# Attention with a sliding window: V held in small array tiles, its product turned on VectorE, and corner masks as products

## The chip, the cores and the metric

One core of one Trainium2 chip runs the whole kernel. The metric is device time in microseconds, the median of several executions; lower is better. The kernel before took 478.73 us (median of three, 477.96 to 478.87).

## What is computed

Two layers over 2048 rows of 512 features. Each layer is an attention block and a dense block, both with a residual and a layer norm ahead of them:

```python
def _A_ref(x, wqkv, wo):                 # H = 32 heads of Dh = 16, window W = 256
    qkv = (x @ wqkv).reshape(B, S, 3, H, Dh)   # then q, k, v as (B, H, S, Dh)
    scores = einsum("bhqd,bhkd->bhqk", q, k) * Dh ** -0.5
    mask = (q_index - k_index >= 0) & (q_index - k_index < W)
    p = softmax(where(mask, scores, -1e9))
    return einsum("bhqk,bhkd->bhqd", p, v)  # heads joined again, then @ wo

def _B_ref(x, w1, w2):                   # Dff = 1792
    return maximum(x @ w1, 0) @ w2

x = x + _A_ref(layernorm(x), wqkv, wo)
x = x + _B_ref(layernorm(x), w1, w2)     # and both once more
```

Inputs and result are bf16; sums are kept in fp32.

## The kernel before, in words

The work goes in eight steps `k`, four chunks of 512 rows for each of the two layers. A step has a norm and q, k, v (`plan_qkv`), attention (`plan_attention`), the projection with `wo`, a second norm and the dense block (`plan_rest`).

**Attention.** The 32 heads are taken in four sets `t` of eight; the eight are four pairs `p` (or `r`) of two heads `e`. A `Unit` is one set over the 512 queries of a step, 28 of them in all; step 0 has eight half units of 256 queries instead. Keys and queries are cut into blocks of 64. A query block sees five key blocks (fewer at the start of the sequence), so a full unit away from the start has 40 pairs of a key block and a query block; all units together have 1200. The tables `FULL`, `HALF` and `BARE` pack these pairs into groups: an entry `(kb, lo, n, at)` is key block `kb` with the `n` query blocks from `lo` on, laid at column `64 * at`. All units together have 372 such entries.

A group is one step of a pipeline. `score_group` makes four matmuls per entry, each on 32 rows of the array (a pair `r`), whose stationary operand `KBD` holds the keys of both heads, so that the result `Sps` has two times 64 keys in its 128 partitions and the queries in its columns. `Sps` fills four PSUM banks and there is one of it, so the scores of the next group wait for the exponential of this one. `exp_group` writes the exponentials to `Pb` (line 418), of which there are two, used by every second unit. Corners, the blocks that the window cuts in a triangle, are set to zero by `mask` (line 422): VectorE takes the minimum with a triangle of 0 and 3e38, a pair of corners in one instruction; GpSimd makes a select for each corner and each head, so four for a pair. All units together have 480 corners.

`pv_group` (line 445) is the attention product. The stationary operand is a 128x128 piece of `Pb` (two heads by 64 keys, 128 queries), the moving one is `V2` with 34 columns: 16 features and a one for each of the two heads, with zeros where the other head's keys lie. The sums build up over up to six key blocks in `acc`, with queries in the partitions; the columns of ones give the softmax sums. A unit is done in pieces of 256 queries, each with one PSUM bank. `divide` (line 453) takes reciprocals of the sums and writes the quotients to `O`. When all four sets of a step are done, four DMA transposes from SP's queue turn `O` into `OT` (in the last step TensorE does it), and `wo` is applied. `accumulate_check` (line 462) keeps whether a reciprocal lay outside fixed bounds; a slow exact path at the end of the program runs if one did.

**The order of the work** is worked out when the program is built. Each piece of work is an `Op` with its engines, a duration for each of them written in the source, what it depends on, and the PSUM bank or buffer it takes (`psum`, four banks, for everything but the scores). A list scheduler walks through time: an idle engine takes the ready piece with the lowest key (for TensorE the key alone; for the others the time since when it is ready, plus a key). Scores come first on TensorE, then the attention product, then the projection, then the dense matmuls by their due times. Where two engines can do a piece (masks: VectorE or GpSimd; evacuations of PSUM: VectorE or ScalarE), the one that is idle first takes it. ScalarE takes other work only if it ends before the next exponential is due (`act_free`). If TensorE has been idle for 0.81 us, a filler matmul (`warm`) is put in. Every engine then runs its instructions in the order so found; the durations in the source only make the order. As every instruction is issued through one helper, nearly all have line 150 in the profile, so they are told apart by tile names.

Of the kernel before, what the change touches and what calls it, by code (L numbers as in the profile page):

```python
# [14 lines left out]
ALU = mybir.AluOpType  # L15
# [24 lines left out]
PW = 576  # L40
# [36 lines left out]
SHOW = None  # L77


class Unit:  # L80


    def __init__(self, k, c, t, q0, nq):
# [4 lines left out]
        self.place = {(kb, q // 2): (g, lo, at) for g, blocks in enumerate(self.groups) for kb, lo, n, at in blocks  # L88
                      for q in range(lo, lo + n)}
# [17 lines left out]
def kernel(  # L107
# [22 lines left out]
    BIG = 3.0e38  # L130
# [75 lines left out]
    Pb = [const.tile([P, PWALL + 64], BF16, name=f"Pb{i}") for i in range(2)]  # L206
    badacc = const.tile([P, 1], FP32, name="badacc")
# [59 lines left out]
    def op(key, opts, deps=(), take=None, uses=(), keep=0):  # L267
        uses = list(uses) + ([take] if take is not None and take not in uses else [])
        return Op(key, opts, deps, take, uses, keep)
# [4 lines left out]
    ots = Pool("OT", 3, work)  # L274

    def landed(t):
        o = Op(0, {}, [], None, [], 0)
        fixed.append((o, t))
        return o
# [116 lines left out]
    def spread_v(e, layer, c, j, src):  # L396
        v4 = src.rearrange("p (a e d) -> p e a d", e=2, d=16)
        for half in range(2):
            sl = slot(layer, 8 * c + 2 * j + half)
            for p in range(2):  # L400
                copy(e, V2[64 * p:64 * p + 64, sl, p, :, 0:16], v4[64 * half:64 * half + 64, p])
# [13 lines left out]
    def places(pb, g):  # L415
        return Pb[pb][:, 0:PWALL].rearrange("p (g r c) -> p g r c", g=5, r=4)[:, g]

    def exp_group(u, g, pb, Sps):
        a, z = bounds(u, g)
        act.activation(places(pb, g)[:, :, 64 + a:64 + z], Sps[:, :, a:z], ACT.Exp, scale=0.25)  # L420

    def mask(e, m, pv4):
        if e == "POOL":
            for at, far in m:
                for h in range(2):
                    v = pv4[64 * h:64 * h + 64, :, 64 + 64 * at:128 + 64 * at]
                    pool.affine_select(out=v, in_=v, pattern=[[0, 4], [-1 if far else 1, 64]],
                                       compare_op=ALU.is_gt if far else ALU.is_ge, fill=0.0, base=0,
                                       channel_multiplier=1 if far else -1)
            return  # L430
        at, k0 = m[0]
        if len(m) == 1:
            v = pv4[:, :, 64 + 64 * at:128 + 64 * at]
            w = tri[:, k0:k0 + 1, :].to_broadcast([P, 4, 64])
        else:
            st, k1 = m[1][0] - at, m[1][1]
            b = pv4[:, :, 64 + 64 * at:128 + 64 * at]
# [4 lines left out]
    def seen(u, jl):  # L442
# [584 lines left out]
```

## Time and profile before

| | |
|---|---|
| median of three runs | 478.73 us (477.96 to 478.87) |
| span of the profiled execution | 474.6 us (its time around the span is not given) |
| busy in the span: TensorE, VectorE, ScalarE, GpSimd | 451.7, 348.1, 345.9, 299.4 us |
| instructions | 14227 |

The span runs from the first to the last instruction of the profiled execution. PE is TensorE's matmuls, PEld its weight loads, DVE VectorE, ACT ScalarE, POOL GpSimd, SP SyncE; a queue of an engine has a q behind it. A row of a group of instructions gives engine, operation, tiles (out<-in), shapes, the count, busy time and the mean duration of one in ns, then the engine's idle time before them and what ended it. Matmuls overlap, so their mean duration holds a latency that a row of them pays once.

### The profile page before, as it was taken

To read this page: it belongs to the slowest core of one execution; us is meant where nothing else is said; L and a number is where in the kernel's file an instruction comes from. 1 tells how busy PE (TensorE), PEld (TensorE's weight loads), DVE (VectorE), ACT (ScalarE), POOL (GpSimd) and SP (SyncE) were. 2 spreads that over 40 slices of the span, in tenths; PEclk is the share of its full clock that TensorE was granted. 3 is DMA by queue.
4 is the path that set the end of the run, shared out by engine and by line. 5 is a ranking of instruction groups with operands and counts; after the bars stand their busy time and mean duration, and the time that the engine had idled before them with its cause. 6 is when DMAs were issued, how large, how long until landed. Compare 5 with 4: busy or idle time off the path is not lost.

```text
span 474.6 us, 14227 instructions
## 1 busy us (share of the span) xinstructions
PE 451.7 (95%) x5890; PEld 242.8 (51%) x5963; DVE 348.1 (73%) x845; ACT 345.9 (73%) x277; POOL 299.4 (63%) x664
## 2 busy tenths in 40 slices
PE   6988999999999999999999999999999999999994
PEld 2654556554555554545454555455555555644443
DVE  6898997887896689767979866898779766461101
ACT  1887987887889778887788787888788788444330
POOL 7587678786797678666887576687767756410000
PEclk9999999999999999999999999999999999999999
DMA  8617122013111112002232022020242002100101
GB/s 267 244 35 192 23 46 48 1 35 47 26 32 36 23 36 46 3 1 47 44 48 35 14 46 46 1 48 3 41 73 46 12 15 35 46 12 11 35 12 39
DMA packets 54807, 21.96 MB, mean 46 GB/s; under 512 B 46160, under 2 KB 54224, under 8 KB 54736
## 3 DMA queue, kind: packets, MB, share of 16 engines
q1 hardware_dynamic: 54736, 20.98, 19.9%
q8 instruction: 48, 0.79, 0.7%
q14 instruction: 23, 0.19, 0.1%
HBM read 7.86 MB, written 2.10 MB: 21 GB/s over the span
## 4 chain that ended last, share of the span: by engine, by line
PE 82%; ACT 5%; DVE 5%; DMA 3%; issue 3%; POOL 2%; SPq 0%; ACTq 0%; DVEq 0%; POOLq 0%
PE ps_d L150 59%; PE acc L150 13%; PE Sps L150 9%; ACT Pb L150 4%; DMA OT<-O 2%; DVE V2f L150 1%; POOL Pb L150 1%; DMA xnT<-xn 1%; DMA x_sb<-in_A_x_dram 1%; PE tp L150 1%; DVE st L150 1%; DVE Pb L150 0%; DVE Vst L150 0%; POOL rstds L150 0%; DVE xn L150 0%
## 5 line engine op out<-in xcount | busy, mean ns | idle before, releaser
L150 ACT ACTIVATE Pb<-Sps 128x2048 bf16<-128x2048 f32 (+2 forms) x156 | 282.6, 1811 | 66.9 <-PE Sps L150 52.2
L150 POOL TENSOR_SCALAR_AFFINE_SELECT Pb<-Pb 64x256 bf16<-64x256 bf16 x504 | 221.8, 440 | 98.5 <-ACT Pb L150 72.2
L150 PE MATMUL ps_d<-xn2T,w 128*128 128x512 bf16 (+1 forms) x485 | 104.7, 355 | 1.6 <-issue 0.8
L150 PE MATMUL ps_d<-w,hT 128*128 128x512 bf16 (+1 forms) x438 | 103.5, 373 | 2.1 <-issue 1.4
L150 PEld LDWEIGHTS <-Pb 128*128 128x128 bf16 x2880 | 82.9, 96 | 21.3 <-issue 9.4
L150 PE MATMUL acc<-V2f,Pb 128*128 128x34 bf16 x2880 | 88.3, 178 | 0.7 <-POOL Pb L150 0.3
L150 DVE TENSOR_TENSOR Pb<-Pb,tri 128x256 bf16<-128x256 bf16 (+1 forms) x143 | 59.9, 429 | 16.9 <-ACT Pb L150 15.6
L150 PEld LDWEIGHTS <-w 128*128 128x128 bf16 x504 | 45.9, 98 | 44.2 <-issue 4.2
L150 PE MATMUL ps_d<-xnT,wqkv 128*128 128x512 bf16 (+1 forms) x275 | 63.3, 355 | 2.3 <-DMA xnT<-xn 1.2
L150 PEld LDWEIGHTS <-hT 128*128 128x128 bf16 x462 | 42.1, 98 | 45.5 <-issue 4.2
L150 PE MATMUL Sps<-Qt,KBD 32*128 32x320 bf16 (+3 forms) x1488 | 60.9, 251 | 3.9 <-ACT Pb L150 3.0
L150 DVE TENSOR_SCALAR hT<-ps_d 128x512 bf16<-128x512 f32 (+1 forms) x66 | 39.6, 607 | 16.4 <-PE ps_d L150 15.7
L150 ACT ACTIVATE hT<-ps_d 128x512 bf16<-128x512 f32 (+1 forms) x60 | 33.9, 568 | 23.5 <-PE ps_d L150 22.2
L150 PEld LDWEIGHTS <-KBD 32*128 32x128 bf16 x1488 | 23.4, 92 | 51.9 <-issue 49.0
L150 DVE TENSOR_SCALAR KBD<-ps_d,par 128x256 bf16<-128x256 f32 (+1 forms) x80 | 44.0, 601 | 1.6 <-PE ps_d L150 1.3
L150 DVE BATCH_NORM_STATS2 st<-x_sb 128x6 f32<-128x512 f32 (+1 forms) x64 | 43.7, 683 | 1.0 <-DMA x_sb<-in_A_x_dram 0.7
L150 DVE TENSOR_TENSOR x_sb<-ps_d,x_sb 128x512 f32<-128x512 f32 x48 | 32.4, 683 | 10.4 <-PE ps_d L150 9.3
L150 PEld LDWEIGHTS <-wqkv 128*128 128x128 bf16 x288 | 25.3, 97 | 25.3 <-issue 4.8
L150 DVE TENSOR_TENSOR ob<-ps_d,x_sb 128x512 bf16<-128x512 f32 (+1 forms) x17 | 11.2, 659 | 32.8 <-PE ps_d L150 32.2
L150 POOL TENSOR_TENSOR rstds<-rstds,mhalf 128x2 f32<-128x2 f32 (+1 forms) x33 | 24.3, 739 | 16.4 <-DVE rstds L150 13.5
L150 DVE TENSOR_SCALAR xn<-x_sb,mvs,rstds 128x512 bf16<-128x512 f32 (+1 forms) x45 | 25.0, 575 | 13.2 <-issue 9.3
L150 PE MATMUL ps_d<-wo,OT 128*128 128x512 bf16 x118 | 31.3, 380 | 1.9 <-DMA OT<-O 1.2
(56 smaller groups left out, 285.1 us busy)
## 6 DMA issues: line engine op xcount, KB each, us to landing
out_dram<-ob SPq DMA_DIRECT2D x15, 128.0 KB, 1.7
w<-in_B_w_dram SPq DMA_DIRECT2D x1, 1792.0 KB, 12.0
w<-in_B_w_dram SPq DMA_DIRECT2D x2, 896.0 KB, 6.4
wqkv<-in_A_wqkv_dram SPq DMA_DIRECT2D x3, 512.0 KB, 7.1
x_sb<-in_A_x_dram SPq DMA_DIRECT2D x3, 512.0 KB, 9.0
x_sb<-in_A_x_dram SPq DMA_DIRECT2D x2, 256.0 KB, 3.0
wo<-in_A_wo_dram SPq DMA_DIRECT2D x1, 512.0 KB, 8.8
xnT<-xn SPq DMA_TRANSPOSE x28, 2.5
```

The source lines that it names most:

```text
L150: inst = fn(*a, **k)
```

## The change

The attention product is turned round: V is the stationary operand, in tiles of 64 rows by 32 columns of the array, one for each of the eight heads of a set, and the exponentials are the moving operand, with up to 320 columns. The result has features in its partitions (for each of four pairs 32, of which 17 are used) and queries in its columns, in two PSUM banks, one for each `e`; a unit takes both at once and is done in one piece. VectorE turns both banks in blocks of 32x32 into fp32 tiles in SBUF, takes reciprocals and the quotients, and turns the quotients back into `OT`, whose layout is that of the transposed `O`; `O`, its DMA transposes and TensorE's transposes in the last step go. GpSimd masks as VectorE does, a pair of corners in one instruction; both multiply by a triangle of 0 and 1. The check now compares each reciprocal with both bounds, so that one that is not a number counts as bad. `V2` needs no zeros and `Pb` no padding any more. The scheduler can take two banks for one piece of work. The durations in the source are changed with the operations; its table of offsets (`TUNE`) is not.

```diff
-PW = 576
+PW = 512
...
-    V2f = const.tile([P, NSLOT * 544], BF16, name="V2f")
-    V2 = V2f[:].rearrange("p (s e a d) -> p s e a d", s=NSLOT, e=2, a=16)
+    V2f = const.tile([P, NSLOT, 288], BF16, name="V2f")
+    V2 = V2f[:, :, 0:272].rearrange("p s (a d) -> p s a d", d=17)
...
     def mask(e, m, pv4):
-        if e == "POOL":
-            for at, far in m:
-                for h in range(2):
-                    v = pv4[64 * h:64 * h + 64, :, 64 + 64 * at:128 + 64 * at]
-                    pool.affine_select(out=v, in_=v, pattern=[[0, 4], [-1 if far else 1, 64]],
-                                       compare_op=ALU.is_gt if far else ALU.is_ge, fill=0.0, base=0,
-                                       channel_multiplier=1 if far else -1)
-            return
...
-        dve.tensor_tensor(out=v, in0=v, in1=w, op=ALU.min)
+        (pool if e == "POOL" else dve).tensor_tensor(out=v, in0=v, in1=w, op=ALU.mult)
...
+    def pv_group(u, g, pb, accs, first, last):
+        for i, (kb, lo, n, at) in enumerate(u.groups[g]):
+            sl = slot(u.k // NCH, 8 * u.c + u.q0 + kb)
+            for p in range(4):
+                col = (4 * g + p) * PW + 64 * at
+                for e in range(2):
+                    rows = slice(64 * e, 64 * e + 64)
+                    h = 17 * (4 * u.t + p)
+                    pe.matmul(accs[e].ps[32 * p:32 * p + 32, 64 * lo:64 * (lo + n)], lhsT=V2f[rows, sl, h:h + 32],
+                              rhs=Pb[pb][rows, col:col + 64 * n], start=first and i == 0,
+                              stop=last and i == len(u.groups[g]) - 1, skip_group_check=True)
+
+    def divide(e_, u, turned, rinv, o):
+        nb = 2 * u.nq
+        v = turned.rearrange("p e (b c) -> p e b c", c=32)[:, :, 0:nb]
+        dve.reciprocal(rinv, v[:, :, :, 16])
+        (pool if e_ == "POOL" else dve).tensor_tensor(
+            out=o[:, 0:64 * u.nq].rearrange("p (b e d) -> p e b d", e=2, d=16), in0=v[:, :, :, 0:16],
+            in1=rinv.rearrange("p e (b o) -> p e b o", o=1).to_broadcast([P, 2, nb, 16]), op=ALU.mult)
...
+        g1 = small.tile([P, P], FP32, name="chk_g1", bufs=1)
+        dve.tensor_scalar(out=g1[:], in0=chk2, scalar1=c_lo, scalar2=None, op0=ALU.is_ge)
+        dve.scalar_tensor_tensor(out=g1[:], in0=chk2, scalar=c_hi, in1=g1[:], op0=ALU.is_le, op1=ALU.mult)
+        mn = goodacc if first else small.tile([P, 1], FP32, name="chk_mn")
+        dve.tensor_reduce(out=mn[:], in_=g1[:], axis=AX.X, op=ALU.min)
...
-                    times = {"DVE": 0.36 + 0.12 * (len(m) - 1), "POOL": 0.98 * len(m)}
+                    times = {"DVE": 0.36 + 0.12 * (len(m) - 1), "POOL": 0.14 + 0.56 * len(m)}
...
+            accs = [Box(psum), Box(psum)]
+            prior, need = None, []
+            for g in range(len(u.groups)):
+                need += [exps[first_slot[n] + g]] + masks[first_slot[n] + g]
...
+            for g in range(len(u.groups)):
...
+                us = sum(b[2] for b in u.groups[g]) * 0.0268 + 0.01 * len(u.groups[g])
+                prior = op(-5e4 + n - (1000 if g else 0), {"PE": (us + (0 if g else 0.1), pfn)},
+                           [prior] if g else need, accs if g == 0 else None, accs)
...
+            for e in range(2):
+                def trfn(e=e, tb=tb, accs=accs, w=w):
+                    if e == 0:
+                        tb.t = tb.tile([P, 2, 512], FP32, "TR")
+                    dve.transpose(out=tb.t[:, e, 0:w], in_=accs[e].ps[:, 0:w])
+                turns.append(op(soon("div", u.k), {"DVE": (0.13 + 0.00105 * w, trfn)}, [prior] + turns, tb if e == 0 else None, [tb, accs[e]]))
...
+                divide("DVE", u, tb.t[:], rinv, ob.t[:])
+            r1 = op(soon("div", u.k), {"DVE": (0.25 + 0.0168 * 2 * u.nq + 0.00105 * w, mufn)}, turns + checks[k - 2:k - 1], ob, [tb])
...
+                dve.transpose(out=ot[:, u.t, q0:q0 + w], in_=ob.t[:, 0:w])
+            m1 = op(soon("div", u.k), {"DVE": (0.13 + 0.00105 * w, bkfn)}, [r1] + wo_mm.get(k - 2, []), None, [ob])
...
-                t = op(-5, {"SP": (1.22, lambda j=j, to=to: sp.dma_start_transpose(
-                    out=to(), in_=O_of[k][:, j, :].rearrange("p (kc d) -> p kc d", kc=KC)), 2.9)}, ready, ob, [ob])
-            turned[k, j] = t
...
-            def womm(kc, ps, ob=ob):
-                mm(ps[:], ob.t[:, kc, :], wo[:, kc, :], kc == 0, kc == KC - 1)
-            box, m = group(-10000 + k, KC, 0.216, womm, [t, d_wo])
+            def womm(kc, ps, j=j):
+                mm(ps[:], OTs[k][:, kc, j * P:(j + 1) * P], wo[:, kc, :], kc == 0, kc == KC - 1)
+            box, m = group(-10000 + k, KC, 0.216, womm, [d_wo] + [divs[k, t, j] for t in range(4)])
```

## Rows read from the trace of the kernel before

**Rows 1.** The page: span, busy engines, chain by engine, two groups of instructions.

```profile
span 474.6 us, 14227 instructions
...
PE 451.7 (95%) x5890; PEld 242.8 (51%) x5963; DVE 348.1 (73%) x845; ACT 345.9 (73%) x277; POOL 299.4 (63%) x664
...
PE 82%; ACT 5%; DVE 5%; DMA 3%; issue 3%; POOL 2%; SPq 0%; ACTq 0%; DVEq 0%; POOLq 0%
...
L150 ACT ACTIVATE Pb<-Sps 128x2048 bf16<-128x2048 f32 (+2 forms) x156 | 282.6, 1811 | 66.9 <-PE Sps L150 52.2
...
L150 PE MATMUL Sps<-Qt,KBD 32*128 32x320 bf16 (+3 forms) x1488 | 60.9, 251 | 3.9 <-ACT Pb L150 3.0
```

**Rows 2.** Stretches: length, busy PE, PEld, DVE, ACT, POOL, clock, DMA share, GB/s.

```profile
14.00:60.00 46.00, 41.11 (x635) 24.39 (x641) 42.45 (x110) 38.67 (x40) 33.32 (x76) 1.00 0.42 111
60.00:408.00 348.00, 339.92 (x4812) 182.79 (x4867) 278.09 (x664) 282.99 (x197) 253.49 (x562) 1.00 0.18 33
408.00:474.60 66.60, 60.38 (x399) 30.96 (x403) 18.60 (x44) 20.41 (x35) 4.13 (x7) 0.99 0.07 24
```

**Rows 3.** The chain that ended last, from 300 to 311 us, by line.

```profile
by line: PE ps_d L150 60.9%; PE acc L150 23.7%; PE Sps L150 14.9%; issue 2.0%
```

**Rows 4.** Timeline of ScalarE: the first and the last exponential (start, length).

```profile
14.05 0.81 ACT L150 ACTIVATE Pb<-Sps 128x768 bf16<-128x768 f32 x1 [0.67 <-PE Sps L150]
...
406.35 1.88 ACT L150 ACTIVATE Pb<-Sps 128x2048 bf16<-128x2048 f32 x1 [0.71 <-PE Sps L150]
```

**Rows 5.** Waits: engine and tile, what it waited for, total, times, longest.

```profile
PE Sps L150 <- ACT Pb L150: 3.0, 10, 0.6
```

**Rows 6.** Timeline after the last exponential, of TensorE and of VectorE.

```profile
414.05 1.89 PE L150 MATMUL ps_d<-wo,OT 128*128 128x512 bf16 x8
...
419.26 12.25 PE L150 MATMUL ps_d<-xn2T,w 128*128 128x512 bf16 x55
...
444.32 12.25 PE L150 MATMUL ps_d<-xn2T,w 128*128 128x512 bf16 x55
...
422.14 1.45 DVE L150 TENSOR_SCALAR xn<-x_sb,mvs,rstds 128x512 bf16<-128x512 f32 x3
...
468.73 0.42 DVE L150 TENSOR_TENSOR ob<-ps_d,x_sb 128x256 bf16<-128x256 f32 x1 [1.10 <-PE ps_d L150]
```

**Rows 7.** Groups of instructions by line and form: count, busy us, mean ns.

```profile
L150 POOL TENSOR_SCALAR_AFFINE_SELECT Pb<-Pb 64x256 bf16<-64x256 bf16 x504 | 221.8, 440 | 98.5 <-ACT Pb L150 72.2 <-DVE O L150 3.0 <-DVE rstds L150 2.5
...
L150 PE MATMUL acc<-V2f,Pb 128*128 128x34 bf16 x2880 | 88.3, 178 | 0.7 <-POOL Pb L150 0.3 <-DVE Vst L150 0.2
...
L150 DVE TENSOR_TENSOR Pb<-Pb,tri 128x512 bf16<-128x512 bf16 x85 | 39.5, 472 | 15.3 <-ACT Pb L150 14.1
...
L150 DVE TENSOR_SCALAR hT<-ps_d 128x512 bf16<-128x512 f32 x46 | 31.7, 690 | 15.0 <-PE ps_d L150 14.5 <-PE Sps L150 0.2
...
L150 DVE TENSOR_TENSOR O<-acc,chk 128x256 bf16<-128x256 f32 x64 | 27.2, 424 | 2.2
...
L150 DVE RECIPROCAL chk<-acc 128x16 f32<-128x16 f32 x64 | 16.2, 253 | 15.9 <-PE acc L150 15.4
...
L150 PE MATMUL Sps<-Qt,KBD 32*128 32x64 bf16 x256 | 13.1, 193 | 0.5 <-ACT Pb L150 0.5
...
L150 POOL TENSOR_SCALAR xn<-x_sb,rstds,nbs 128x512 bf16<-128x512 bf16 x5 | 3.9, 787 | 0.5
```

**Rows 8.** Timeline of TensorE from 200.5 to 203.3 us.

```profile
200.72 0.31 PE L150 MATMUL acc<-V2f,Pb 128*128 128x34 bf16 x6
200.96 0.40 PE L150 MATMUL Sps<-Qt,KBD 32*128 32x320 bf16 x8
201.28 1.82 PE L150 MATMUL acc<-V2f,Pb 128*128 128x34 bf16 x66
```

**Rows 9.** Timeline of TensorE from 405.5 to 406.5 us.

```profile
405.85 0.40 PE L150 MATMUL Sps<-Qt,KBD 32*128 32x64 bf16 x12
```

**Rows 10.** The chain from 110 to 121 us, in order of time.

```profile
112.35 4.61 DMA OT<-O
```

More of the change, by code (lines that the diff above doesn't have):

```diff
@@ L77 @@
 SHOW = None
+DRY = False
 class Unit:
@@ L267, in op @@
     def op(key, opts, deps=(), take=None, uses=(), keep=0):
-        uses = list(uses) + ([take] if take is not None and take not in uses else [])
+        take = [] if take is None else take if isinstance(take, list) else [take]
+        uses = list(uses) + [b for b in take if b not in uses]
         return Op(key, opts, deps, take, uses, keep)
@@ L273 @@
     stg = Pool("stg", 3, work)
-    ots = Pool("OT", 3, work)
+    trs = Pool("tr", 2, work)
+    ons = Pool("on", 2, work)
     def landed(t):
-        o = Op(0, {}, [], None, [], 0)
+        o = Op(0, {}, [], [], [], 0)
         fixed.append((o, t))
@@ L477 @@
+        dve.tensor_scalar(out=g1[:], in0=chk2, scalar1=c_lo, scalar2=None, op0=ALU.is_ge)
+        dve.scalar_tensor_tensor(out=g1[:], in0=chk2, scalar=c_hi, in1=g1[:], op0=ALU.is_le, op1=ALU.mult)
+        mn = goodacc if first else small.tile([P, 1], FP32, name="chk_mn")
+        dve.tensor_reduce(out=mn[:], in_=g1[:], axis=AX.X, op=ALU.min)
+        if not first:
+            dve.tensor_tensor(out=goodacc[:], in0=goodacc[:], in1=mn[:], op=ALU.min)
     out_v = out.rearrange("b (n p) d -> p (b n) d", p=P)
@@ L546, in plan_qkv @@
         old = [scores[s] for n in units_of.get(k - 2, []) for s in range(first_slot[n], first_slot[n] + len(units[n].groups))]
-        old_pv = [pvs[n, j] for n in units_of.get(k - 2, []) for j in range(units[n].nq // 2)]
+        old_pv = [pvs[n] for n in units_of.get(k - 2, [])]
         wait = 0 if k == 0 else tune("wait", k, 16)
@@ L599, in plan_attention @@
             pb = n % 2
-            before = [pvs[n - 2, j] for j in range(units[n - 2].nq // 2)] if n > 1 else [c_p[0], c_p[1]]
+            before = [pvs[n - 2]] if n > 1 else []
             for g in range(len(u.groups)):
@@ new lines, in plan_attention, with mufn, bkfn @@
+            rinv = chks[k % 2][:, u.t, 4 * u.q0:4 * u.q0 + 4 * u.nq].rearrange("p (e b) -> p e b", e=2)
+            def mufn(u=u, tb=tb, ob=ob, rinv=rinv):
+                ob.t = ob.tile([P, 512], BF16, "ON")
+                divide("DVE", u, tb.t[:], rinv, ob.t[:])
+            r1 = op(soon("div", u.k), {"DVE": (0.25 + 0.0168 * 2 * u.nq + 0.00105 * w, mufn)}, turns + checks[k - 2:k - 1], ob, [tb])
+            recips.setdefault(k, []).append(r1)
+            def bkfn(u=u, ob=ob, w=w, q0=q0):
+                ot = first(OTs, u.k, lambda: work.tile([P, KC, 512], BF16, name="OT", tag=f"OT{u.k % 2}", bufs=1))
+                dve.transpose(out=ot[:, u.t, q0:q0 + w], in_=ob.t[:, 0:w])
@@ L793, in choose @@
         for at, o in ready[e]:
-            if at > t + 1e-9 or (o.take is not None and sum(1 for f, _ in o.take.pool.free if f <= t + 1e-9) <= o.keep):
+            if at > t + 1e-9 or (o.take and sum(1 for f, _ in o.take[0].pool.free if f <= t + 1e-9) < len(o.take) + o.keep):
                 continue
@@ L815, in begin @@
             ready[x] = [r for r in ready[x] if r[1] is not o]
-        if o.take is not None:
-            free = sorted(o.take.pool.free)
-            o.take.index = free[0][1]
-            o.take.pool.free = free[1:]
+        for b in o.take:
+            free = sorted(b.pool.free)
+            b.index = free[0][1]
+            b.pool.free = free[1:]
         us, fn, *total = o.opts[e]
-        o.made = by_name[e].made
-        fn()
+        if not DRY:
+            fn()
         busy[e] = t + us
```

130 lines of the change are left out of this document (35 added, 95 removed).

## The prediction

> **What bounds the kernel now.** I read the page's head first: TensorE is busy 95% of the span, VectorE and ScalarE 73%, GpSimd 63%, and the chain that ended last is 82% TensorE [rows 1]. The stretches by time come second. They part the span into three: a start (14 to 60 us) in which VectorE is the fullest engine (42.45 of 46 us, 92%; TensorE 41.11), a long middle in which TensorE works 339.92 of 348 us and VectorE 278.09, and a tail after 408 us in which VectorE has 18.60 us of work and TensorE 60.38 [rows 2]. The third view is the chain inside an ordinary stretch of the middle: it is all TensorE, 60.9% dense matmuls (`ps_d`), 23.7% the attention product (`acc`), 14.9% scores (`Sps`) [rows 3].
>
> There is a second chain beside it. ScalarE runs 156 exponentials, the first at 14.05 us, the last ending at 406.35 + 1.88 = 408.2 us [rows 1, 4]: one each 2.53 us, of which 1.88 us is the operation and the rest is the score group between two of them, which must wait for the exponential before it. TensorE waited for them there only 3.0 us in all [rows 5]. So in the middle the exponentials keep their pace, the dense work fills the gaps between score groups, and what doesn't fit piles up behind the last exponential: from 419.26 to 444.32 us TensorE does the whole feed-forward of step 6, and only then that of step 7, which closes the kernel [rows 6]. That pile is what a cheaper attention product can shrink.
>
> **The change, part by part.** *Attention product on TensorE.* Before: 2880 matmuls of 34 columns; 66 of them last 1.82 us of which one latency is 0.178, so 1.64 / 66 = 24.9 ns each [rows 7, 8], 71.7 us in all. After: each block of `groups` becomes 8 matmuls (4 column tiles by 2 row tiles) with 64n columns. The blocks are those of the scores, which run as 4 row tiles: 1488 / 4 = 372 blocks [rows 1], and their 1200 pairs of key and query block have 1200 · 64 = 76,800 columns, as many as 150 groups of 512. How fast small tiles go side by side is shown by the scores: 8 matmuls (192 and 320 columns) and 12 matmuls (64, 128 and 320) both last 0.40 us [rows 8, 9]; less the latency of about 0.17 (a 64-column matmul's 193 ns [rows 7] less 27 ns of columns at 2.4 GHz, the level granted here) that is 0.23 us for 512 columns per tile, whatever the number of matmuls and weight loads. I take this for the new product: 150 · 0.23 = 35 us. Changing the array's shape costs about 0.09 us each way: the last of 6 `acc` matmuls starts at 200.72 + 5 · 0.025 = 200.85, its columns are through at 200.86, the scores start at 200.96; coming back, score columns end about 201.19 and `acc` starts at 201.28 [rows 8]. Thirty-six units enter and leave the new shape: at most 36 · 0.18 = 6.5 us. Sum 41.5 us, a saving of 30 us of TensorE. Bounds: below, columns alone (76,800 / 2.4 GHz = 32 us); above, `acc`'s 24.9 ns for each of 2976 matmuls, 74 + 6.5 = 81 us. No row shows column tiles side by side; I take the scores' value because they are tiles of the same array with the same blocks.
>
> *VectorE.* Gone are 64 reciprocals (0.253) and 64 products (0.424) [rows 7]: 1.354 us for a unit of 512 queries, 0.677 for a half one. New for a full unit: two transposes of 512 fp32 columns out of PSUM, one reciprocal of 32, one product of 512, one transpose back of 512 bf16. No transpose on VectorE is in the trace. The nearest rows are 0.690 for 512 fp32 out of PSUM and 0.472 for 512 bf16 in a mask [rows 7]. I take 0.69 for each transpose and for the product, since two of the three transposes read fp32 from PSUM as that row does, and 0.38 for the reciprocal: 3.14 us, 1.79 more than before. For a half unit 0.42 each (the old product, 256 fp32) and 0.25: 1.93, 1.25 more. 28 · 1.79 + 8 · 1.25 = 60 us. Bounds: 40 us with transposes at 0.47 (0.3 for half units), about 130 if a transposed column cost double. The new check has four operations of about the same size in place of five: nothing.
>
> *GpSimd.* A pair of corners was four selects of 0.440, 1.76 us; 504 of them are 222 us for 252 corners. Now it is one product of 128x512 with two inputs. Below: 0.787, one input of that size on GpSimd; above: 1.57, the two read in turn [rows 7]. I take 1.2, 151 us, 70 less. The Trainium skill (GPSIMD Engine Reference, Performance versus the Vector engine) has 4497 ns for a two-input sum of 2048; scaled that is an estimate of 1.12 us, with which this term would be 141 us. What GpSimd gains may take masks from VectorE (85 pairs at 0.472): I count 40 pairs, 19 us. ScalarE also has room in the gaps between exponentials, some 12 us of evacuations. VectorE's net growth is about 30 us; before 408 us it then does 42.45 + 278.09 + 30 = 350 us in 394, 89%, still under the 92% it holds in the start.
>
> *SP and the transposes.* 28 of the DMA transposes of `O` leave SP's queue; one stood on the chain with 4.61 us at 112 [rows 10]. The VectorE path that takes their place is about as long (two transposes, reciprocal, product, transpose: 3.3 us with gaps). I count 3 us for such stalls. TensorE's own 16 transposes at the end go as well.
>
> *Banks.* The product now takes two of four PSUM banks at once. Unshown; below nothing, above one evacuation (0.69) a unit, 25 us of TensorE waiting. I take nothing, because TensorE gains more slack than that. What waits behind a transpose that waits for its product is VectorE's next work, masks and evacuations, and behind these TensorE; before, the reciprocal waited for `acc` in the same place.
>
> *Start.* VectorE is 92% full from 14 to 60 us and the eight half units add 10 us there; GpSimd's selects there get a third cheaper and can take some of it back. I take 4 us, between nothing and 10.
>
> **The sum.** Exponentials end at 408.2 + 4 - 3 = 409 us. Behind them: mask 0.47, product 1.35, VectorE 3.3, so that the projection starts 5.1 us later, at 413.3 by the old times, where it now starts at 414.05. From there the old rows give three normalised tiles at 422.14 + 1.45 = 423.6 and the fourth about 0.5 later, transposed about 425; step 7's feed-forward takes 468.73 - 444.32 = 24.4 us and the end from there 474.6 - 468.73 = 5.9 [rows 6]. 425 + 24.4 + 5.9 = 455.3, a tail of 47 us in place of 66.4. It needs the pile gone: about 30 us of dense work, of which some 11 fit into TensorE's idle time between 408 and 425; the other 19 must move forward into the 29 us that the product frees. It fits. Span 409 + 47 = 456. The median of the runs stands 4.1 us over the span (478.73 - 474.6; the profiled execution's time around its span isn't given otherwise): **460 us**. The range of this case is 450 to 468: five us less if looser TensorE shortens the gaps between exponentials, more if masks and evacuations come late.
>
> **Rivals.** *VectorE becomes the bound.* For it: the start is already its stretch, and planned costs, not measured ones, decide what moves to GpSimd and ScalarE; against it: both have room. With nothing moved it does 320.5 + 58 = 379 us before the last exponential; at 92% that is 412 us, exponentials end at 426, and the time is 426 + 47 + 4 = 477. GpSimd's product costing no less than its selects leads here too.
>
> *Array tiles don't run side by side: slower.* Price: 81 us for the product instead of 71.7, TensorE stays the bound, 478.7 + 9 = 488. It decides from 0.175 us per set of eight on (65.2 us over 372 sets, with the changes of shape). Against it: the scores' 12 loads and 12 matmuls in 0.40 us; for it: eight loads per block instead of four, in column tiles, which no row shows. The Trainium skill (TensorE: Matmul & The Clock Gate, Part 3, What overlaps and what doesn't) says that a weight load overlaps running matmuls only if its row group differs; by it each set of eight would load after its predecessor. The scores' three sets on the same rows, in the time of two, speak against that rule [rows 8, 9].
>
> *The freed time isn't used.* The dense work stays where the planner puts it, behind the last exponential, TensorE idles or runs filler in the middle, and the tail stays 66 us: 475 to 479. Against it: the planner starts any ready matmul on an idle TensorE.
>
> **How the numbers follow.** My case 0.57, VectorE 0.17, tiles 0.13, unused time 0.09, other mishaps 0.04. A measurement of this kernel can tell 0.2% (1 us) from no change. Faster: 0.57, most of the second and two thirds of the fourth, 0.75; same 0.05; slower: the third, a part of the second and the mishaps, 0.20. The range 448 to 482 takes in the first two cases and the fourth and leaves out the tiles case and the tails.
>
> **What would show it.** Right: 2976 `acc` matmuls whose unit lasts about 1.3 us of TensorE; 108 VectorE transposes of about 0.69 and 0.42; GpSimd products of about 1.2 us; exponentials still 2.5 us apart; step 6's feed-forward mostly ahead of the last exponential and a tail near 47 us. Wrong: a unit's product of 2 us or more, VectorE at over 92% between 60 and 400 us with exponentials spaced wider, or many filler matmuls ahead of an unchanged tail.

## The result: 484.32 us where 460 was forecast

The changed kernel took 484.32 us (median, 482.28 to 485.2), beside 478.35 us for the kernel before on the same chip: a ratio of 1.0132, 95% interval 1.0097 to 1.0167. It is slower by 1.3%, outside of the predicted range. The profiled execution has a span of 483.5 us. The page of its profile answers to [rows 1]:

```profile
span 483.5 us, 14096 instructions
...
PE 437.3 (90%) x6014; PEld 204.5 (42%) x6081; DVE 410.8 (85%) x811; ACT 336.9 (70%) x267; POOL 291.6 (60%) x394
...
PE 51%; DVE 37%; DMA 3%; issue 3%; POOL 2%; ACT 2%; SPq 0%; DVEq 0%; ACTq 0%; POOLq 0%
...
L148 PE MATMUL acc<-Pb,V2f 64*32 64x320 bf16 (+4 forms) x2976 | 45.9, 251 | 1.1 <-POOL Pb L148 0.5
```

TensorE did get relief: 437.3 us busy in place of 451.7, although 11.6 us more of it are filler (`warm`: 74 matmuls of 22.9 us in all, before 36 of 11.3). Its granted clock was 0.991 over the span, before 0.999; an estimate from that, 0.8% of 437 us, gives it 3.5 us of the loss at most. But VectorE went from 348.1 to 410.8 us, 33 us beyond the 378 that the prediction comes to, and the chain that ended last is now 37% VectorE where it was 5%. The stretches (columns as in [rows 2]) say where:

```profile
14.00:60.00 46.00, 38.82 (x658) 20.00 (x665) 43.99 (x102) 36.14 (x39) 33.90 (x51) 0.96 0.36 108
60.00:408.00 348.00, 320.24 (x4634) 147.03 (x4683) 322.01 (x615) 263.91 (x192) 238.01 (x315) 1.00 0.12 23
408.00:483.50 75.50, 67.67 (x678) 32.40 (x683) 37.39 (x71) 32.56 (x32) 16.05 (x15) 0.99 0.06 20
```

In the middle VectorE works 322.01 of 348 us, 92.5%, fuller than TensorE: the sign that the prediction named for its being wrong. The exponentials fall behind: the last ends at 433.88 + 1.88 = 435.8 us (before 408.2 [rows 4], forecast 409).

```profile
433.88 1.88 ACT L148 ACTIVATE Pb<-Sps 128x2048 bf16<-128x2048 f32 x1 [0.72 <-PE Sps L148]
```

From there the kernel needs 47.7 us, against 47 forecast: this number came out, for a reason that is taken up below; the exponentials' did not. The groups by form show which of VectorE's and GpSimd's operations are dearer than the rows before them [rows 7] (busy time, mean ns). Two rows of the kernel before that don't stand there:

```profile
L150 DVE COPY V2f<-Vst 64x256 bf16<-64x256 bf16 x76 | 26.9, 354 | 1.0
...
L150 DVE TENSOR_TENSOR Pb<-Pb,tri 128x256 bf16<-128x256 bf16 x58 | 21.0, 364 | 1.6 <-ACT Pb L150 1.5
```

and those of the changed kernel:

```profile
L148 POOL TENSOR_TENSOR Pb<-Pb,tri 128x512 bf16<-128x512 bf16 x138 | 163.2, 1189 | 118.8 <-ACT Pb L148 116.0 <-DVE TR L148 1.6
L148 DVE STREAM_TRANSPOSE TR<-acc 128x512 f32<-128x512 f32 x56 | 37.4, 695 | 6.5 <-PE acc L148 6.4
L148 DVE TENSOR_TENSOR Pb<-Pb,tri 128x512 bf16<-128x512 bf16 x66 | 37.0, 567 | 10.9 <-ACT Pb L148 10.6
L148 DVE TENSOR_TENSOR ON<-TR,chk 128x512 bf16<-128x512 f32 x28 | 26.1, 932 | 1.0
L148 DVE COPY V2f<-Vst 64x256 bf16<-64x256 bf16 x48 | 23.5, 490 | 0.6
L148 DVE STREAM_TRANSPOSE OT<-ON 128x512 bf16<-128x512 bf16 x28 | 19.7, 703 | 0.5
L148 DVE TENSOR_TENSOR Pb<-Pb,tri 128x256 bf16<-128x256 bf16 x34 | 18.6, 548 | 0.1
L148 DVE STREAM_TRANSPOSE TR<-acc 128x256 f32<-128x256 f32 x16 | 6.4, 421 | 0.0
```

The new operations out of PSUM cost what was taken. But VectorE's own masks, not touched but for `min` to `mult`, went from 472 to 567 ns (full) and from 364 to 548 (half), its copies of V from 354 to 490, and the quotients last 932 ns where 690 was taken. One place shows the cause at work. The chain from 252 to 258 us (start, length):

```profile
253.21 0.23 DVE V2f L148
...
253.88 0.44 DVE V2f L148
...
255.20 1.21 DVE V2f L148
...
256.43 1.10 DVE V2f L148
```

and the timeline of GpSimd, TensorE and ScalarE from 252 to 268 us:

```profile
253.38 1.71 POOL L148 COPY V2f<-Vst 64x256 bf16<-64x256 bf16 x4
...
255.18 3.37 POOL L148 TENSOR_TENSOR Pb<-Pb,tri 128x512 bf16<-128x512 bf16 x3
...
259.01 4.67 PE L148 MATMUL ps_d<-xn2T,w 128*128 128x512 bf16 x20 [1.31 <-DVE KBD L148]
...
265.34 1.11 PE L148 MATMUL acc<-Pb,V2f 64*32 64x320 bf16 x72
...
265.87 1.66 ACT L148 ACTIVATE Pb<-Sps 128x1792 bf16<-128x1792 f32 x1 [9.24 <-PE acc L148]
```

The same copy of V takes VectorE 0.23 us where GpSimd's own copies only just begin, 0.44 us beside these, and 1.21 and 1.10 us beside GpSimd's products: each of the two ends within 0.1 us of the end of a product. And a second thing: the last mask of the unit is done at 255.18 + 3.37 = 258.55 us at the latest, yet its product starts only at 265.34 us. TensorE did dense matmuls in between, each group of which takes one bank when one comes free. That two banks were therefore never free at once is inferred here, and e3_hold tests it. The exponential needs the `Pb` that this product reads and waits 9.24 us: 11.61 us from one exponential to the next, the longest distance in the run.

### The profile page after: what moved, and what is told of

It reads as the page before. It is cut to its first block, busy times and chain, and to the rows that moved or that the text cites. A ratio compares the mean times of both kernels' runs of the same rounds, so it can differ in the third digit from the quotient of the medians.

```text
span 483.5 us, 14096 instructions
## 1 busy us (share of the span) xinstructions
PE 437.3 (90%) x6014; PEld 204.5 (42%) x6081; DVE 410.8 (85%) x811; ACT 336.9 (70%) x267; POOL 291.6 (60%) x394
## 4 chain that ended last, share of the span: by engine, by line
PE 51%; DVE 37%; DMA 3%; issue 3%; POOL 2%; ACT 2%; SPq 0%; DVEq 0%; ACTq 0%; POOLq 0%
PE ps_d L148 39%; PE Sps L148 6%; PE acc L148 5%; DVE st L148 5%; DVE KBD L148 5%; DVE x_sb L148 4%; DVE V2f L148 3%; DVE Pb L148 3%; DVE TR L148 3%; DVE ON L148 2%; ACT Pb L148 2%; DMA wqkv<-in_A_wqkv_dram 2%; DVE xn L148 2%; DVE mvs L148 2%; PE warm L148 1%
## 5 line engine op out<-in xcount | busy, mean ns | idle before, releaser
L148 POOL TENSOR_TENSOR Pb<-Pb,tri 128x512 bf16<-128x512 bf16 (+1 forms) x176 | 192.0, 1104 | 127.7 <-ACT Pb L148 124.8
L148 DVE TENSOR_TENSOR Pb<-Pb,tri 128x512 bf16<-128x512 bf16 (+1 forms) x100 | 55.1, 560 | 11.0 <-ACT Pb L148 10.6
L148 DVE TENSOR_SCALAR KBD<-ps_d,par 128x256 bf16<-128x256 f32 (+1 forms) x86 | 46.9, 594 | 3.6 <-PE ps_d L148 3.5
L148 DVE STREAM_TRANSPOSE TR<-acc 128x512 f32<-128x512 f32 (+1 forms) x72 | 43.8, 634 | 6.5 <-PE acc L148 6.4
L148 PE MATMUL acc<-Pb,V2f 64*32 64x320 bf16 (+4 forms) x2976 | 45.9, 251 | 1.1 <-POOL Pb L148 0.5
L148 DVE TENSOR_SCALAR hT<-ps_d 128x512 bf16<-128x512 f32 (+1 forms) x71 | 42.2, 622 | 4.6 <-PE ps_d L148 4.4
L148 PEld LDWEIGHTS <-V2f 64*32 64x32 bf16 x2976 | 34.5, 91 | 17.0 <-issue 11.6
L148 ACT ACTIVATE hT<-ps_d 128x512 bf16<-128x512 f32 (+1 forms) x55 | 29.4, 542 | 8.9 <-PE ps_d L148 8.3
L148 POOL COPY V2f<-Vst 64x256 bf16<-64x256 bf16 x76 | 32.7, 430 | 3.6 <-DVE Vst L148 1.0
L148 PE MATMUL ps_d<-wqkv,xnT 128*128 128x512 bf16 x120 | 30.9, 380 | 3.4 <-DMA wqkv<-in_A_wqkv_dram 1.9
```

Source lines behind the costliest of these rows:

```text
L148: inst = fn(*a, **k)
```

## The experiments

Two theories stood after the result. **Held-up work:** a GpSimd product with two inputs from SBUF holds up VectorE's operations between SBUF operands, and VectorE became the bound. **Banks:** the product that wants two banks starves behind dense groups that want one. A third came in on the way: **the order**, since any edit of the source's durations makes the list scheduler find another one.

**e1_selects: GpSimd's selects put back into the changed kernel.**

```diff
+        if e == "POOL":
...
+                    pool.affine_select(out=v, in_=v, pattern=[[0, 4], [-1 if far else 1, 64]],
...
-        (pool if e == "POOL" else dve).tensor_tensor(out=v, in0=v, in1=w, op=ALU.mult)
+        dve.tensor_tensor(out=v, in0=v, in1=w, op=ALU.mult)
...
-                    times = {"DVE": 0.36 + 0.12 * (len(m) - 1), "POOL": 0.14 + 0.56 * len(m)}
+                    times = {"DVE": 0.36 + 0.12 * (len(m) - 1), "POOL": 0.98 * len(m)}
```

> The changed kernel with GpSimd's four selects per pair of corners put back (planned at 0.98 us a corner as before); everything else as changed. Shared reads (GpSimd's two-input products hold up VectorE's operations that read SBUF): VectorE's mask pair falls from 0.567 to about 0.47, its quotient product of 512 from 0.932 to about 0.69, VectorE loses 30 us or more of busy time, and the time falls to 474 to 479 although GpSimd itself gets slower. Banks (the product waits for two free banks while dense groups take each one as it comes free): the stall of about 10 us in the middle stays, time within 3 us of 484. Volume (VectorE's 60 us of new work alone sets the pace): 484 or more, since GpSimd then takes fewer masks.

475.16 us, ratio 0.994 [0.9914, 0.9967]: 9 us back. VectorE's full masks fall to 477 ns, the quotients to 754, its total to 383.8 us. A stall of 12.35 us between two exponentials (at 244 us) stays, so it is not the held-up work that makes it.

**e2_products: the kernel before with the new mask alone**: GpSimd's selects go, both engines multiply by a triangle of 0 and 1, and the planned duration is that of the changed kernel.

```diff
-        dve.tensor_tensor(out=v, in0=v, in1=w, op=ALU.min)
+        (pool if e == "POOL" else dve).tensor_tensor(out=v, in0=v, in1=w, op=ALU.mult)
...
-                    times = {"DVE": 0.36 + 0.12 * (len(m) - 1), "POOL": 0.98 * len(m)}
+                    times = {"DVE": 0.36 + 0.12 * (len(m) - 1), "POOL": 0.14 + 0.56 * len(m)}
```

> The kernel before with one part of the change alone: GpSimd masks a pair of corners by one product, both engines multiply by a 0/1 triangle, with the changed planned cost. Shared reads: VectorE's mask pair rises from 0.472 to 0.55 or more and its copies of V from 0.354 to 0.45 or more; 3 to 6 us slower than before, 481 to 485. Banks and volume: GpSimd does less work and VectorE keeps its durations, so 475 to 479, not slower.

486.22 us, ratio 1.0161 [1.012, 1.0203]. Masks on VectorE go from 472 and 364 ns to 539 and 667, copies of V from 354 to 430: the new mask alone loses 8.3 us in the old kernel. It holds up VectorE without any transposes there. The old quotients, whose sums come from PSUM and only the reciprocals from SBUF, are not held up: 425 ns, before 424.

**e3_hold: the scheduler keeps banks for a product that is ready.**

```diff
+        held = [o.key for at, o in ready[e] if e == "PE" and len(o.take) == 2 and at <= t + 1e-9]
...
+            if held and o.take and o.key > min(held):
+                continue
```

> The changed kernel; only the scheduler differs: while an attention product is ready and waits for its two banks, no dense group takes a bank. Banks: the exponentials lose their stall of 11.6 us, the last one ends some 9 us earlier, and the time is 472 to 476. Shared reads and volume: VectorE sets the pace as before, the time stays within 3 us of 484.

479.19 us, ratio 1.0015 [0.9987, 1.0043]: 5.1 us back, less than the theory of the banks alone needs. The long stall is gone (the longest distance of exponentials is 5.0 us); VectorE is as full as before (408.9 us).

**e4_hold_noback: e3_hold without the transposes back.** `divide` writes straight to `OT`; the turning back of the quotients is left out.

> As the run that holds banks, and the transpose back of the quotients is left out (the quotients are written where the turned ones would be, so the projection reads them unturned): 36 VectorE operations and 23 us of VectorE less. Volume: 8 to 15 us less than the run that holds banks. Banks: within 2 us of it. Shared reads: within 4 us of it, since the mask and quotient operations that are held up remain.

468.58 us, ratio 0.9807 [0.9763, 0.9852], VectorE 396.1 us: 13 us of VectorE's time off, 10.6 us of the kernel's. That fits a kernel whose time VectorE's volume sets; but this is another order than e3_hold's, and orders alone move that kernel by 6.4 us (below).

**e5_hold_selects: e3_hold with the selects of e1_selects.**

> The changed kernel with both repairs: GpSimd's selects back and banks held for a ready attention product. If shared reads and banks are two separate losses, their gains add: 484.3 less 9 (selects alone) less 5 (holding alone) gives 468 to 472, faster than both kernels, and the stall of 12 us in the middle is gone. If VectorE's volume has become the only bound once the selects are back, holding adds nothing: 474 to 477.

467.75 us, ratio 0.9804 [0.9775, 0.9832]. Both repairs together give 16.6 us, about what the two gave singly (9.2 and 5.1).

**e6_one_input: e3_hold with GpSimd's product taken with a constant instead of the triangle.** Its durations in the plan are not changed, so every engine runs the same order as in e3_hold; GpSimd's masking is left out.

```diff
-        (pool if e == "POOL" else dve).tensor_tensor(out=v, in0=v, in1=w, op=ALU.mult)
+        if e == "POOL":
+            pool.tensor_scalar(out=v, in0=v, scalar1=1.0, scalar2=None, op0=ALU.mult)
+            return
+        dve.tensor_tensor(out=v, in0=v, in1=w, op=ALU.mult)
```

> As the run that holds banks, same order of all work, but GpSimd's product with the triangle is replaced by a product of the same tile with the constant 1 (one input read instead of two); this leaves out the masking of the corners that GpSimd had. If it is the second input that holds VectorE up: VectorE's mask pair falls from 0.647 to about 0.47, its quotient product from 0.893 to about 0.70, and the time falls by 6 to 12 us against the run that holds banks. If any long GpSimd instruction on the same tiles does it: mask pair above 0.58 and time within 3 us.

467.14 us, ratio 0.9777 [0.9756, 0.9798]. The groups by form of e3_hold:

```profile
L148 POOL TENSOR_TENSOR Pb<-Pb,tri 128x512 bf16<-128x512 bf16 x138 | 166.0, 1209 | 109.7 <-ACT Pb L148 108.5
L148 DVE TENSOR_TENSOR Pb<-Pb,tri 128x512 bf16<-128x512 bf16 x66 | 42.4, 647 | 7.3 <-ACT Pb L148 7.1
L148 DVE TENSOR_TENSOR ON<-TR,chk 128x512 bf16<-128x512 f32 x28 | 25.0, 893 | 1.0
L148 DVE TENSOR_TENSOR Pb<-Pb,tri 128x256 bf16<-128x256 bf16 x31 | 17.3, 557 | 0.1
```

and of e6_one_input:

```profile
L148 POOL TENSOR_SCALAR Pb<-Pb 128x512 bf16<-128x512 bf16 x138 | 209.1, 1523 | 58.6 <-ACT Pb L148 56.7 <-PE acc L148 0.6
L148 DVE TENSOR_TENSOR Pb<-Pb,tri 128x512 bf16<-128x512 bf16 x66 | 33.2, 507 | 10.2 <-ACT Pb L148 10.0
L148 DVE TENSOR_TENSOR ON<-TR,chk 128x512 bf16<-128x512 f32 x28 | 20.7, 738 | 1.0
L148 DVE TENSOR_TENSOR Pb<-Pb,tri 128x256 bf16<-128x256 bf16 x31 | 10.4, 334 | 0.3 <-ACT Pb L148 0.2
```

GpSimd's operation became longer (1523 ns for 1209), and yet the same 66 masks of VectorE fell from 647 to 507 ns. VectorE's total fell by 31.3 us to 377.6, and the time by 12.0 us, in one and the same order. So it is not the length of GpSimd's operation that makes most of the hold-up, but its second input from SBUF (or something else in which GpSimd's `tensor_tensor` differs from its `tensor_scalar`; no run parts the two). This is the cleanest measurement of the loss, though in one order.

The second input is not all of it. Each instruction of VectorE can be put under the work of GpSimd that ran beside it longest. The traces of e3_hold and e6_one_input then give these means in ns, the longest in brackets:

| VectorE's operation | GpSimd idle (e3_hold) | beside its product of two inputs (e3_hold) | beside its product of one input (e6_one_input) |
|---|---|---|---|
| full mask | 406 | 782 (1406) | 521 (866) |
| quotients of 512 | 692 | 981 (1564) | 756 (1099) |
| copy of V | 230 | 692 (1217) | 393 (685) |
| transpose of 512 out of PSUM | 699 | 697 (718) | 700 (718) |

One input holds VectorE up as well, by less. The selects did so in the kernel before: a copy of V took 231 ns there with GpSimd idle and 390 beside selects, and the row's 354 is the mean over all.

**e7_measured: e3_hold, products kept, with measured durations in the plan** (as they are while GpSimd's products run).

```diff
-                    times = {"DVE": 0.36 + 0.12 * (len(m) - 1), "POOL": 0.14 + 0.56 * len(m)}
+                    times = {"DVE": 0.56 + 0.09 * (len(m) - 1), "POOL": 0.3 + 0.46 * len(m)}
```

and likewise the quotients (0.25 to 0.5), V's copies on VectorE (1.35 to 1.75) and the norm (0.6 to 0.8, 0.22 to 0.38).

> As the run that holds banks, GpSimd's products kept, but the scheduler's durations set to what the held-up operations took (VectorE mask pair 0.65, single 0.56, quotients 0.25 us longer, V copies 1.75 for four, norm 0.8; GpSimd pair 1.22). Wrong order: a plan that knows the durations gains back half of the loss, 470 to 475. Held-up work itself (shared reads): the operations are just as long in any order, so within 3 us of the run that holds banks.

466.43 us, ratio 0.9764 [0.9744, 0.9783], the fastest version with the whole computation. The operations are held up as much as ever (quotients 991 ns), but a plan that knows it gives VectorE less, 384.7 us, and wins more than the half that was expected. Its page:

```profile
span 466.2 us, 14103 instructions
...
PE 436.0 (94%) x6055; PEld 203.3 (44%) x6055; DVE 384.7 (83%) x761; ACT 349.3 (75%) x294; POOL 311.8 (67%) x415
...
PE 68%; DVE 13%; ACT 10%; POOL 4%; issue 2%; DMA 2%; SPq 0%; ACTq 0%; POOLq 0%; DVEq 0%
```

The exponentials end where the prediction had them (409), but the tail behind them is not the 47 us of the prediction: 466.2 - 408.9 = 57.3 us. The last exponential, and the middle with the columns of [rows 2]:

```profile
406.99 1.88 ACT L148 ACTIVATE Pb<-Sps 128x2048 bf16<-128x2048 f32 x1 [0.71 <-PE Sps L148]
...
60.00:408.00 348.00, 334.04 (x4956) 153.22 (x4946) 314.06 (x590) 290.28 (x223) 266.91 (x340) 1.00 0.13 24
```

**e8_measured_nohold: e7_measured without the held banks.**

> The changed kernel with the measured durations in the scheduler, banks not held. If knowing the durations is what gave the run with both its 466 us: 465 to 470 here too. If holding banks is needed beside it: the order so found has attention products waiting for two banks, two gaps of over 12 us between exponentials, and the time is 482 to 494.

489.17 us, ratio 1.0235 [1.0206, 1.0264], 22.7 us more than with them. Two exponentials come 16.93 and 13.40 us after the one before. The first, in the timelines of GpSimd, TensorE and ScalarE:

```profile
58.40 0.67 POOL L148 TENSOR_TENSOR Pb<-Pb,tri 128x256 bf16<-128x256 bf16 x1
...
63.05 6.72 PE L148 MATMUL ps_d<-xn2T,w 128*128 128x256 bf16 x44 [0.72 <-DVE KBD L148]
...
72.07 0.85 PE L148 MATMUL acc<-Pb,V2f 64*32 64x192 bf16 x64
...
55.68 1.02 ACT L148 ACTIVATE Pb<-Sps 128x1024 bf16<-128x1024 f32 x1
...
72.61 1.88 ACT L148 ACTIVATE Pb<-Sps 128x2048 bf16<-128x2048 f32 x1 [15.42 <-issue]
```

The masks are done at 59.07 us, and the product starts 13 us later, behind dense groups.

**e9_products_measured: e2_products with those durations.**

> The kernel before with GpSimd's products alone, as in the run of that part, with the measured durations of the held-up operations in the scheduler. Wrong order: 476 to 481, at most 1% over the kernel before, against 486.2 with the durations unknown. Held-up work itself: 484 to 488. VectorE's mask operations stay at 0.54 us and more in both cases.

480.18 us, ratio 1.0056 [1.004, 1.0072]: the plan wins back 6.0 of the 8.3 us.

**e10_measured_noback: e7_measured without the transposes back.**

> The kernel of e7_measured (466.4 us) with the transposes back left out: the quotients are written to the output tile as they stand, so this run leaves out the turning back of the result, some 17 us of VectorE's work. If VectorE's volume still sets the time as it did in e4_hold_noback (10.6 us less), 456 to 460 us, and the last exponential ends 6 us or more before the 408.9 of e7_measured. If TensorE has become the bound again, as its 68% of the chain of waits says, within 3 us of 466.4, and VectorE's busy time falls by 17 us to some 368 without a use.

463.59 us, ratio 0.9705 [0.9673, 0.9737]: 2.8 us less than e7_measured, and the last exponential ends at 412.4 us, not earlier than its 408.9. But VectorE's busy time fell by 5.2 us, not by the 17 that were left out:

```profile
PE 436.1 (94%) x6054; PEld 202.7 (44%) x6054; DVE 379.5 (82%) x745; ACT 342.9 (74%) x280; POOL 303.1 (65%) x407
```

The order found here gave VectorE 13 masks and 11 evacuations of `hT` more. So this run doesn't say what 17 us of VectorE's work are worth with both repairs. That its volume no longer sets the time is suggested by e14_measured_nudge below, where VectorE has 394.3 us of work, 9.6 more than in e7_measured, in the same time.

**e11_selects_measured: held banks, selects, and the durations of that mixture.**

> All three repairs: banks held, GpSimd's masks as selects (448 ns each in e1_selects), and the measured durations of the work that stays in the plan. If TensorE is the bound again after either of the two repairs of VectorE's load, the third adds nothing: 464 to 468 us, beside 467.75 for e5_hold_selects and 466.43 for e7_measured. If VectorE's volume still sets the time wherever it is held up, taking the hold-up away as well gives 5 to 8 us more: 458 to 462 us.

481.53 us, ratio 1.0071 [1.0044, 1.0098]: neither theory. VectorE has only 374.3 us of work, yet one exponential comes 11.76 us after the one before. The timelines of TensorE and GpSimd:

```profile
105.01 3.84 PE L148 MATMUL warm<-ident 128*128 128x512 bf16 x17
...
113.08 1.89 PE L148 MATMUL ps_d<-xnT,wqkv 128*128 128x512 bf16 x7 [2.09 <-DMA xnT<-xn]
...
107.78 1.05 POOL L148 TENSOR_SCALAR xn<-x_sb,rstds,nbs 128x512 bf16<-128x512 bf16 x1
```

GpSimd normalises a tile late, among its selects; the DMA transpose behind it lands as late; TensorE runs filler and then waits for it. What it waits for is a DMA, not a bank. This run raised the question how far all these numbers hang on the order.

**e12 to e18: the same kernels in other orders.** A planned duration makes nothing but the order. One was moved by 0.03 us, up in e12 to e16 and down in e17 and e18: that of a transpose out of the banks, or in the kernel before that of reciprocal and quotients. From e12_after_nudge:

```diff
-                turns.append(op(soon("div", u.k), {"DVE": (0.13 + 0.00105 * w, trfn)}, [prior] + turns, tb if e == 0 else None, [tb, accs[e]]))
+                turns.append(op(soon("div", u.k), {"DVE": (0.16 + 0.00105 * w, trfn)}, [prior] + turns, tb if e == 0 else None, [tb, accs[e]]))
```

What was expected, from e12 to e18 in turn:

> The changed kernel (484.3 us) with one duration of the plan raised by 0.03 us, that of a transpose out of the banks, to what it lasts in the trace (0.695 us): no work is changed, only the order that the scheduler finds. If the loss belongs to the change, 480 to 488 us. If the loss was one unlucky order, the time scatters by 8 us or more and may fall to 476 us or less.

> The same 0.03 us in e3_hold (479.2 us). If orders of one kind agree within 3 us, 476 to 482 us, so that the 5.1 us of holding the banks are an effect. If orders scatter by more, outside of it, and the 5.1 us are not told from chance.

> The same 0.03 us in e7_measured (466.4 us). If the 12.8 us gained there belong to the measured durations, 464 to 470 us. If they were a lucky order, 472 us or more.

> The same 0.03 us in e11_selects_measured (481.5 us, with one stall of 11.76 us between two exponentials that no other run has). If that stall was one unlucky order, 464 to 471 us; if selects with these durations always put the normalised tiles too late behind GpSimd's selects, 476 us or more with a stall over 5 us again.

> The kernel before (478.0 us) with one planned duration, that of the reciprocal and quotients, raised by 0.03 us: only the order differs. If its offsets are fitted to its order, 481 us or more, and the change is to be compared with such an order. If orders of the kernel before agree, 476 to 480 us.

> The same duration lowered by 0.03 us. As for e16_before_nudge: 481 us or more if the old order is a fitted one, 476 to 480 us if not.

> The changed kernel with the planned duration of a transpose out of the banks lowered by 0.03 us: a third order of it, beside 484.3 us as it stands and 473.65 us in e12_after_nudge. If the order as it stands is an unlucky one of a group near 474, 470 to 478 us. If orders of this kernel scatter evenly over 10 us, 478 to 486 us.

| kernel | as first run | other orders |
|---|---|---|
| before | 478.35 | 479.77 (e16), 477.65 (e17) |
| changed | 484.32 | 473.65 (e12), 480.08 (e18) |
| banks held (e3_hold) | 479.19 | 472.82 (e13) |
| held, measured durations (e7_measured) | 466.43 | 466.64 (e14) |
| held, measured, selects (e11_selects_measured) | 481.53 | 473.50 (e15) |

The orders of the kernel before lie within 2.1 us, those of the changed kernel within 10.7. Their means are 478.6 and 479.4 us: the change is worth nothing that these orders tell apart from zero. e12_after_nudge is faster than before by 1.1% (ratio 0.9894 [0.9861, 0.9928]), and it has no distance of exponentials over 4.6 us: the 11.61 us of the changed kernel's own order, 9 more than an ordinary 2.6, would make most of the 10.7 us between them. What all three orders share is VectorE. The page of e12_after_nudge:

```profile
PE 435.3 (92%) x6006; PEld 203.5 (43%) x6071; DVE 403.6 (85%) x802; ACT 343.5 (72%) x279; POOL 286.0 (60%) x385
...
PE 50%; DVE 39%; ACT 4%; issue 3%; DMA 3%; SPq 0%; POOL 0%; ACTq 0%; DVEq 0%
```

and of e18_after_nudge2:

```profile
PE 439.7 (91%) x6019; PEld 205.1 (43%) x6085; DVE 405.9 (84%) x808; ACT 339.2 (70%) x267; POOL 289.7 (60%) x379
...
DVE 46%; PE 39%; DMA 5%; issue 3%; POOL 3%; ACT 2%; SPq 0%; DVEq 0%; POOLq 0%; ACTq 0%
```

e15_selects_nudge, at 473.50 us, has no long stall either (4.8 us at most) and lies between its two expectations. So the 5.1 us of e3_hold (6.4 us lie between its own two orders) and the 9.2 of e1_selects are not sizes to rely on, nor are the 10.6 of e4_hold_noback. Solid are e6_one_input (same order, 12.0 us), the rows of durations, which repeat in every run, and held banks with measured durations, 466.4 and 466.6 us. The selects' 467.75 us in e5_hold_selects did not repeat with other durations. One thing was not tried: the offsets in `TUNE` are those of the kernel before, and offsets fitted to the changed kernel might give it a better order.

## Why the prediction was wrong

Two steps failed above all: "VectorE's net growth is about 30 us", which came to 63, and "Banks", which was taken at nothing. The other steps come first.

**Right: the attention product on TensorE.** 72 matmuls take 1.11 us, one latency of 0.19 in it [rows 7, for the 64-column score], so about 13 ns each and 38 us for 2976, where 35 were taken; the 6.5 us for the changes of shape were not measured by themselves. Without filler TensorE has 26 us less to do (440.4 to 414.4), where 30 were counted. A set of eight takes 0.10 us, and the rival of the tiles decides from 0.175 on: column tiles run side by side, and that its 488 us lie near the measured time is chance. By the rule of the Trainium skill that the prediction cited (TensorE: Matmul & The Clock Gate, Part 3, What overlaps and what doesn't), each set of eight loads after its predecessor. This trace speaks against that as the scores did: a load has 91 ns in its row, and a set with its loads and columns 0.10 us.

**Right: the single new durations.** Transposes 695, 421 and 703 ns (0.69 and 0.42 taken), reciprocal 346 (0.38), GpSimd's product 1189 (1.2). VectorE gave up 43 of 143 masks (19 pairs and 24 single corners), where 40 pairs were counted.

**Right in number, by luck: the tail, 47 us.** It was worked out for exponentials that end at 409 us, on the condition that the dense pile moves forward into TensorE's freed time: "It fits." In the changed kernel the exponentials ended 27 us late, and TensorE had done the pile by then: 142 matmuls of the dense block start behind the last exponential, before 252. In e7_measured, where the exponentials do end at 408.9 us, 221 are still behind, and the tail is 57.3 us (56.5 in e14_measured_nudge). TensorE was busy 334.04 of 348 us in the middle there, little less than before, so most of the pile did not move forward. Why the freed time did not take it was not tried.

**Wrong: the VectorE term, "net growth is about 30 us".** It priced every operation by its row in a trace in which GpSimd made selects. With products on GpSimd those rows no longer hold: the 43 masks fewer saved VectorE 5 us (60.5 to 55.6) in place of 19, the quotients cost 932 ns in place of 690, copies and norms grew too. e6_one_input has VectorE at 377.6 us, near the 378 of the sum. But that agreement is in part chance, since one entry of the sum failed for another reason: ScalarE was to take some 12 us of evacuations, but its `hT` went from 60 operations to 55 and its `KBD` from 8 to 2, and its busy time fell from 345.9 to 336.9 us. In return 28 of VectorE's copies of V went to GpSimd and ScalarE, which the sum did not count. The term is 63 us, not 30, and "350 us in 394" became 366 (43.99 + 322.01), 93%. The rival "VectorE becomes the bound" is what happened; its path was not foreseen, and 0.17 was too little for it.

The Trainium skill (GPSIMD Engine Reference, Key points) states that GpSimd shares its SBUF interfaces with VectorE, and that VectorE's instructions with two SBUF inputs or in a two-port mode contend with it. Its page SBUF — State Buffer (Who interferes with whom) calls that an exclusive lock held for a whole instruction. The masks and quotients of e3_hold (647 and 893 ns) agree with it. e6_one_input agrees only in part: beside a GpSimd operation of 1523 ns that reads one SBUF input the masks and quotients were held up too, but the longest took 866 and 1099 ns, some 460 and 410 more than alone, which is far from a whole instruction; there the measurement decides. The prediction looked up GpSimd's price there and not its effect on the neighbour.

**Wrong: Banks, "I take nothing, because TensorE gains more slack than that".** Slack doesn't help a piece that needs two banks when every bank that comes free goes to a piece that needs one. In the changed kernel there is one stall of 11.61 us, in e1_selects one of 12.35, in e8_measured_nohold two, of 16.93 and 13.40; with banks held all are gone (5.9 us at most, but for the stall of e11_selects_measured, which has another cause). Not every order without held banks has one: e12_after_nudge and e18_after_nudge2 have none (6.6 us at most).

**Wrong: the range.** It knew bounds of prices and none for the order. The sign of the result, slower, belongs to the order that the scheduler found. That most of the 18 us of gain failed to come belongs to VectorE and the banks: with both steps mended (e7_measured, e14_measured_nudge) the change gives 2.4%, about 60% of what was forecast, and the 6.4 us that are still missing there are less than the 10 by which its tail is longer than forecast. A small term was wrong as well: the profiled run of the changed kernel took 485.2 us with a span of 483.5, so that 1.7 us stand around the span and not 4.1, and the sum would have been 458.

Left open: the start (4 us were counted), SP's stalls (3 us for the removed DMA transposes) and the new check (counted as nothing; its operations take 12 us of VectorE, the old ones took 9) were not tried by themselves, and why selects with measured durations lose 6 to 14 us against e5_hold_selects is seen in one stall only.

## What to carry to other kernels

Before work goes to GpSimd, ask whether the new operation reads two inputs from SBUF, and then price VectorE's SBUF operations anew, in the plan's durations too: here that was 31 us of VectorE's time in one order, where the moved masks were to save 19. A resource taken in twos from a pool that others take singly needs a reservation. And where a scheduler makes the order, judge an edit over a few orders: 0.03 us in one duration moved the same work by 10.7 us. A term that comes out should be looked at under the conditions that it was worked out for: the tail of 47 us came out only while the exponentials were late.

## What the runs showed of the hardware

- GpSimd's product with two SBUF inputs stretches VectorE's operations between SBUF operands: masks 507 to 647 ns, quotients 738 to 893 in the same order (longest quotient in the changed kernel 1675). A GpSimd product with one input stretches them less: masks 521 beside it, 406 with GpSimd idle. VectorE's old quotients, with one input from PSUM, are not touched (424 ns before, 425 in e2_products), nor are its transposes, out of PSUM (695 ns in the changed kernel, 698 with selects) or within SBUF (703 and 704).
- On GpSimd one input was slower than two: 1523 ns against 1209 for 128x512 in place, in the same tile.
- A transpose on VectorE costs about the same for bf16 in SBUF (703 ns) as for fp32 out of PSUM (695).
